# Sparse attention with routed experts on one Trainium2 core: all eight PSUM banks given out in the order's own sequence, V in five blocks per head, tokens gathered from the output, a new order

## The chip, the cores and the metric

The kernel runs on one core of one Trainium2 chip. The metric is the device time of one execution in microseconds. Before the change it is 942.32 us, the median of 3 runs (941.84 to 942.96).

## What is computed

Attention of 8 batches and 8 heads over 576 positions with head size 64, in which a score counts only if it lies within tau of its row's maximum; then a layer in which each of the 4608 tokens either passes unchanged or goes to one of 8 experts with two matrices each.

```python
# q, k, v: (8, 8, 576, 64); tau: 0.02
scores = scale * q @ k.T                      # per batch and head
scores = where(scores >= max(scores) - tau, scores, -1e9)
attn = softmax(scores);  x = attn @ v         # tokens: (4608, 512)
do_compute = x @ w_skip > 0
e_idx = argmax(x @ w_gate);  gate_w = softmax(x @ w_gate)[e_idx]
out = x
out[t] += gate_w[t] * (relu(x[t] @ w1[e]) @ w2[e])   # e = e_idx[t], if do_compute[t]
```

## The kernel before

**Stages.** Attention works on pairs of heads: 8 batches of four pairs, 32 pairs in all (g = 0 to 31). A pair has nine steps of 128 query or key positions (four for each head, and one in which the two heads' last 64 positions stand together, the tail). After attention, eight experts and one early part of the first follow as nine jobs (two layers each).

**One pair.** `plan_pair` loads q and k (L501, raw<-in_qk), splits them into a high and a low part (hl, L465/L467 and L522), and `plan_dist` and `plan_blk` spread them by DMA from SBUF to SBUF into QK (L569 to L585) and BD (L557). `plan_score` multiplies scores into PSUM (shp, L743) and takes row maxima on DVE (L748); `plan_thresh` makes the thresholds, which PE turns into rows (L838) and ACT writes into QK (L848). `plan_weights` multiplies the transposed scores less the threshold (sps, L716), takes exp on ACT (L884) and masks on DVE (p, L889); p is split into phh (ACT, L465, or DVE, L467) and phl (POOL, L926). `plan_av` multiplies them with V (avp, L954 to L958), ACT copies the result out (a), POOL divides by the sum (xb, L1006; for the tails x, L1019).

**V.** `plan_v` loads V of one batch in four DMAs (L603), takes its largest magnitude on ACT (L623), scales it (L686), rounds it to 16 bits (Vh, L689) and subtracts the rest on POOL (Vl, L692). Each head has NT = 6 blocks of 64 columns: four of 128 positions, and the last 64 positions twice, once in the lower and once in the upper half of the partitions.

**After a batch.** `plan_rows` stores the tokens of a batch (xb) in four pieces, each twice: into xs, from which the experts gather, and into out (L1125). `plan_tails` does so for the last 64 positions of two batches together (L1136). `plan_logits` makes the gate's logits on PE (L1062, L1088), `plan_gate` ranks the tokens on DVE and scatters records of token and weight into a list in HBM by POOL (lst, L1312).

**PSUM.** PSUM has eight banks of 512 float32 columns. They are dealt out for good: sps is a ring of two tiles of two banks (SPB = 2), shp a ring of two of one bank (SHB = 2), avp and gps have one bank each. The rows of the thresholds take an sps tile.

**The order.** The whole of attention and the start of the first job are not issued as written. `Plan.op` and `Plan.dma` collect operations with their dependences, an estimate of their duration for each engine that could do them and a priority; a ring (`take`, `free`) makes an operation wait for the release of the buffer it reuses. `Plan.place` goes through time greedily and picks for each engine the operation of best priority; `run` repeats that with priorities shaken by each of a list of seeds (SEEDS), each pass from the last one's times. The last pass emits the instructions in that order, and the engines then run it in order with the waits that the dependences need. The estimates know of no clock and of no contention on the DMA engines other than one common link.

**The experts.** For each job `gather_x` copies the list of token numbers (L1739, L1740) and gathers their rows from xs by indirect DMA on POOL (L454); `prep_x` turns them (L1753 to L1755), `layer1` and `layer2` or `layer2_t` multiply in three products of high and low parts (L1771, L1805, L1824), `store` scatters the result into out (L1783). `late_table` prepares a table for a loop that handles experts with more tokens than planned; on these inputs the loop is not entered.

Of the kernel before, what the change touches and what calls it, by code (L numbers as in the profile page):

```python
# [24 lines left out]
P = 128  # L25
S = 576
# [27 lines left out]
NT = NM + 2  # L54
NTP = 2 * NM + 1
STEP = 2 * NM + 1
SPB = 2
# [3 lines left out]
PFB = 3  # L61
# [19 lines left out]
GAL = {"DVE": 0.165, "POOL": 0.0}  # L81
SEEDS = (
# [11 lines left out]
class Op:  # L94
    def __init__(self, key, fn, eng, lat, off, port):
# [3 lines left out]
        self.xfer = ()  # L99

# [14 lines left out]
    def latest(self):  # L115
        r = 0.0
        for s, order in self.succ:
            x = s.rev - self.length() if order else s.rev + self.latency(s.on)
            r = x if x > r else r
        return r  # L120
# [9 lines left out]
class Plan:  # L130
    def __init__(self, tc):
        self.ops, self.rings, self.tc = [], {}, tc
        self.last = None

    def emit(self, o):
# [6 lines left out]
        nc.push_inst_callback(note)  # L142
        o.fn(e) if code.co_argcount and code.co_varnames[0] == "e" else o.fn()
# [45 lines left out]
    def place(self, links, options, ready, rank, put, lag):  # L189
# [3 lines left out]
        wait = [len(a) for a, _ in links]  # L193

# [7 lines left out]
        for _ in links:  # L202
            best = None
            for e in ENGINES:
                c = cand[e]
                if not c:
                    continue
# [9 lines left out]
            free[e] = put(i, e, t, free[e])  # L217
            if e in PEER and e in self.ops[i].port:
# [7 lines left out]

    def forward(self, rank, emit=False):
        link = 0.0

        def put(i, e, t, _):  # L230
# [7 lines left out]
            if emit:  # L238
                self.emit(o)
            return end  # L240

        self.place(self.fore, lambda i: self.opts[i], lambda i, e: self.ops[i].ready(e), rank, put, LAG)
        return max(o.t1 for o in self.ops)

    def backward(self):
        link = 0.0

        def put(i, e, t, was):
# [10 lines left out]
        ops = self.ops  # L259
        self.place(  # L260
            self.back, lambda i: (ops[i].on,), lambda i, e: ops[i].latest(), lambda i, e: -ops[i].t1, put, GAL
# [18 lines left out]
    def run(self, seeds):  # L280
        ops = self.ops
        at = {id(o): i for i, o in enumerate(ops)}
        self.opts = [[e for e in ENGINES if e in o.eng] for o in ops]
# [11 lines left out]
def attn_moe_kernel(ctx: ExitStack, tc: tile.TileContext, qk, vl, tau, wg, w1, w2, out):  # L295
# [14 lines left out]
    xs = dp.tile([NTOK, DM], F32, name="xs")  # L310
# [1770 lines left out]
```

## Time and profile before

| | us |
|---|---|
| median of 3 runs | 942.32 |
| the profiled execution | 938.75 |
| its span, first to last instruction | 937.0 |
| PE busy | 870.6 (93%) |
| DVE busy | 691.5 (74%) |
| POOL busy | 662.2 (71%) |
| ACT busy | 628.7 (67%) |

The profile is of one execution. Busy time of an engine is the time in which at least one of its instructions runs; a matmul counts from its start to its modelled end, so matmuls that follow each other closely overlap, and PE can read as busy while it could take more. Windows of the span are given as A:B in microseconds from its start. The clock is that granted to TensorE, as a share of 2.4 GHz; it has two levels, 1.2 and 2.4 GHz, so a mean between 0.50 and 1.00 is a mixture.

### The profile page before, as it was taken

What the parts mean: (1) busy time and instruction counts of PE and PEld (TensorE: products, weight loads), DVE (VectorE), ACT (ScalarE), POOL (GpSimd) and SP (SyncE); (2) the same over time, 40 slices, a digit from 0 to 9 for tenths busy, and PEclk for the clock granted to TensorE, in tenths of its full rate; (3) what the DMA queues carried; (4) which work ended last, traced back from release to release, by engine and by line L of the source; (5) the groups of instructions that cost most, each with busy time, mean ns of one, the idle gap of its engine ahead of it and who ended that gap; (6) DMA issues with size and microseconds to landing.
All of it is one profiled execution on the core that took longest, in us unless ns stands there. A gap on an engine that the chain in (4) does not pass through costs nothing. (4 is left out here: it accounts for less than half of the span.)

```text
span 937.0 us, 24810 instructions
## 1 busy us (share of the span) xinstructions
PE 870.6 (93%) x9630; PEld 808.6 (86%) x9630; DVE 691.5 (74%) x1622; ACT 628.7 (67%) x947; POOL 662.2 (71%) x452
## 2 busy tenths in 40 slices
PE   6899998998999999999998999978889999999994
PEld 3789997997999998899997898867879898999993
DVE  4888986888888888889895898967525554487770
ACT  1588986886998897899896699768414442455450
POOL 5288884896788898999987799968334545365451
PEclk8799998999999999999997999989989999999998
DMA  7987676669679759877866674623356535544530
GB/s 207 217 224 174 130 202 178 146 164 267 135 156 265 171 110 259 188 160 200 224 147 184 173 168 91 176 91 114 113 162 228 193 102 181 180 144 180 178 115 18
DMA packets 81790, 157.37 MB, mean 168 GB/s; under 512 B 28619, under 2 KB 28875, under 8 KB 81672
## 3 DMA queue, kind: packets, MB, share of 16 engines
q1 hardware_dynamic: 76984, 145.49, 59.4%
q0 software_dynamic: 4544, 10.28, 3.3%
q8 instruction: 77, 1.26, 0.5%
q14 instruction: 41, 0.34, 0.1%
q10 hardware_dynamic: 144, 0.00, 0.0%
HBM read 70.78 MB, written 24.78 MB: 102 GB/s over the span
## 5 line engine op out<-in xcount | busy, mean ns | idle before, releaser
L926 POOL TENSOR_TENSOR phl<-p,phh 128x1152 f16<-128x1152 f32 x128 | 305.4, 2394 | 58.5 <-ACT phh L465 16.1
L748 DVE TENSOR_REDUCE mx<-shp 128x1 f32<-128x288 f32 x558 | 236.7, 448 | 48.7 <-PE shp L743 45.5
L884 ACT ACTIVATE e<-sps,ntau 128x576 f32<-128x576 f32 x288 | 211.0, 740 | 57.4 <-PE sps L716 54.3
L889 DVE SCALAR_TENSOR_TENSOR p<-sps,e 128x576 f32<-128x576 f32 x288 | 215.4, 751 | 33.1 <-ACT e L884 24.9
L743 PE MATMUL shp<-QK 128*128 128x288 f32 x992 | 201.6, 314 | 6.1 <-DVE mx L748 3.2
L716 PE MATMUL sps<-QK 128*128 128x288 f32 x1024 | 191.7, 312 | 10.7 <-ACT QK L848 5.4
L716 PEld LDWEIGHTS sps<-QK 128*128 128x128 f32 x1024 | 148.7, 193 | 19.2 <-ACT QK L848 7.1
L743 PEld LDWEIGHTS shp<-QK 128*128 128x128 f32 x992 | 149.7, 191 | 12.8 <-DVE mx L748 7.8
L465 ACT ACTIVATE phh<-p 128x1152 f16<-128x1152 f32 x117 | 136.4, 1166 | 12.2 <-DVE p L889 8.1
L958 PE MATMUL avp<-Vh,phl 128*128 128x65 f16 x1280 | 130.8, 194 | 7.4 <-POOL phl L926 7.3
L954 PE MATMUL avp<-Vh,phh 128*128 128x65 f16 x1280 | 132.8, 196 | 2.6 <-ACT a L465 2.5
L957 PE MATMUL avp<-Vl,phh 128*128 128x64 f16 x1280 | 131.6, 193 | 0.0
L958 PEld LDWEIGHTS <-phl 128*128 128x128 f16 x1280 | 118.0, 98 | 8.2 <-POOL phl L926 8.1
L954 PEld LDWEIGHTS <-phh 128*128 128x128 f16 x1280 | 116.8, 98 | 8.1
L957 PEld LDWEIGHTS <-phh 128*128 128x128 f16 x1280 | 118.1, 99 | 3.0 <-issue 3.0
L1734 POOL TENSOR_TENSOR wl<-wr,wh 128x1024 fp32r<-128x1024 f32 x28 | 72.5, 2601 | 35.4 <-ACT wh L1733 30.0
L1771 PE MATMUL hps<-xh,wl 128*128 128x256 f32 (+4 forms) x256 | 77.1, 301 | 0.0
L1771 PE MATMUL hps<-xh,wh 128*128 128x256 f32 (+4 forms) x248 | 76.5, 308 | 0.1
L1771 PE MATMUL hps<-xl,wh 128*128 128x256 f32 (+4 forms) x248 | 75.0, 303 | 0.0
L1772 ACT ACTIVATE QK<-hps 128x256 fp32r<-128x256 f32 (+4 forms) x64 | 26.9, 421 | 68.9 <-PE hps L1771 68.2
L1783 POOL DMA_INDIRECT out<-o,ids x21 | 21.0, 1001 | 71.5 <-DVE o L1782 30.0
L692 POOL TENSOR_TENSOR Vl<-vraw,Vh 128x768 f16<-128x768 f32 x32 | 51.0, 1600 | 22.3 <-ACT Vh L689 22.1
(261 smaller groups left out, 1912.1 us busy)
## 6 DMA issues: line engine op xcount, KB each, us to landing
QK<-hl SPq DMA_DIRECT2D x192, 288.0 KB
wr<-in_w SPq DMA_DIRECT2D x31, 1024.0 KB
raw<-in_qk SPq DMA_DIRECT2D x32, 576.0 KB
vraw<-in_vl SPq DMA_DIRECT2D x32, 384.0 KB
xs<-xb SPq DMA_DIRECT2D x32, 256.0 KB
out<-xb SPq DMA_DIRECT2D x32, 256.0 KB
BD<-hl SPq DMA_DIRECT2D x64, 64.0 KB
xs<-x SPq DMA_DIRECT2D x8, 128.0 KB
```

Of the source, the lines that this page charges most:

```text
L465: nc.scalar.activation(dst, src, AF.Copy)
L716: nc.tensor.matmul(ps[:, j, 0:HS], w_, x_[:, js], start=(i == 0), stop=(i == len(mm) - 1))
L743: nc.tensor.matmul(ps[:, 0:HS], w_, x_[:, js], start=(q == 0), stop=(q == len(mm) - 1))
L748: nc.vector.tensor_reduce(T["mx", g][:, o, j : j + 1], T.pop(("S", g, i, j))[:, 0:HS], AX.X, ALU.max)
L884: nc.scalar.activation(e, T["W", g, i][:, :, 0:HS], AF.Exp, bias=ntau, scale=0.125)
L889: nc.vector.scalar_tensor_tensor(T[z][:, kt % 2].rearrange("p (a b) -> p a b", a=2), T.pop(("W", g, i))[:, :, 0:HS], 0.0, T.pop(("e", g, i ...
L926: nc.gpsimd.tensor_tensor(T["pl", g, i], T.pop(z)[:, 0:nk], T["ph", g, i], op=ALU.subtract)
L954: nc.tensor.matmul(pv[:, c, :], x, Vh[:, vh, kt, :], start=(j + q + c == 0), stop=False, skip_group_check=True)
L957: nc.tensor.matmul(pv[:, c, 0:D], x, Vl[:, vh, kt, :], start=False, stop=False, skip_group_check=True)
L958: nc.tensor.matmul(pv[:, c, :], y, Vh[:, vh, kt, :], start=False, stop=(c == NM), skip_group_check=True)
L1734: lo[q % 2].tensor_tensor(w[1][:, sl], rs, w[0][:, sl].bitcast(F32), op=ALU.subtract)
L1771: nc.tensor.matmul(hp_[:, 0:cap], w_, x, start=(i == 0), stop=(i == len(mm) - 1))
```

## The change

**PSUM.** The four pools become one tile of eight banks, `banks`. In `place`, each operation that takes a PSUM buffer gets a free bank, or for sps and the rows two neighbouring ones, at the moment it is placed: that which comes free first. The bank goes back when the operations that read it have been placed. A score pair may now have three instead of two buffers in flight, shp, gps and avp have no limit but the eight banks, and the rows have a kind of their own. The p ring grows from three to four. Instructions are emitted after the last pass, not during it. The backward pass knows who waits for a bank.

**V.** NT is 5: the last 64 positions stand once, in the lower half of the partitions for even heads and the upper half for odd heads.

**Tokens.** The tensor xs is gone with its stores (32 of rows, 8 of tails, one of a constant). The gathers read out. Rows of the list that hold no token are no longer clamped to a valid row: the gather leaves them out, and the two buffers that it first fills are cleared on DVE before. The gathers and the scatters of different experts are declared free of each other. The late loop masks rows that an earlier part has done; `late_table` has six more small operations for that.

**Order.** Durations of the DMAs in the plan are changed, and 50 new seeds give a new order.

```diff
-NT = NM + 2
+NT = NM + 1
-SPB = 2
+SPB = 3
-PFB = 3
+PFB = 4
+SHARED = {"shp": 0, "gps": 0, "avp": 0, "sps": 2, "row": 2}
+BANKS = 8
...
+                if name in SHARED:
+                    o.grab, o.kind = (name, len(al)), SHARED[name]
+                    if al and name == "sps":
+                        o.deps.append((al[-1], True))
+                    if name == "sps" and len(al) >= bufs:
+                        o.deps += [(x, False) for x in fr[len(al) - bufs]]
+                    al.append(o)
+                    continue
+    def open(self, units, e):
+        f = sorted(u[0][e] for u in units if u[1] == 0)
+        two = [max(u[0][e], v[0][e]) for u, v in zip(units, units[1:]) if u[1] == 0 and v[1] == 0]
+        return (f[0] if f else None, f[1] if len(f) > 1 else None, min(two, default=None))
+
+    def hold(self, o, e, units):
...
-    ps_s = att.enter_context(tc.tile_pool(name="ps_s", bufs=SPB, space=PSUM))
-    ps_h = att.enter_context(tc.tile_pool(name="ps_sh", bufs=SHB, space=PSUM))
-    ps_t = att.enter_context(tc.tile_pool(name="ps_t", bufs=1, space=PSUM))
-    ps_a = att.enter_context(tc.tile_pool(name="ps_a", bufs=1, space=PSUM))
+    ps_b = att.enter_context(tc.tile_pool(name="ps_b", bufs=1, space=PSUM))
+    banks = ps_b.tile([P, BANKS, 512], F32, name="banks")
...
-            xs[0:n, :],
+            out[0:n, :],
...
-        nc.sync.dma_start(
-            xs[NTOK - S - TL : NTOK - S, :].rearrange("p (o c) -> p o c", c=P),
-            ident[0:TL].rearrange("p (o c) -> p o c", o=1).broadcast_to([TL, DM // P, P]),
-        )
...
+    def bank():
+        return banks[:, pl.bank[0]]
+
     def sps():
-        return ps_s.tile([P, 2, 512], F32, name="sps", tag="sps")
+        a, b = pl.bank
+        return banks[:, a : b + 1 : b - a]
...
-        r = pl.op(n + OFF["tr"], rows, [o] + ring.take("sps", SPB), {PE: 0.45})
+        r = pl.op(n + OFF["tr"], rows, [o] + ring.take("row", 1), {PE: 0.45})
...
         for t in range(NM):
-            for i, dst in enumerate((xs, out)):
-
-                def st(t=t, dst=dst):
-                    r0 = b * S + t * P
-                    nc.sync.dma_start(dst[r0 : r0 + P, :], T["x", b][:, t, :])
+
+            def st(t=t):
+                r0 = b * S + t * P
+                nc.sync.dma_start(out[r0 : r0 + P, :], T["x", b][:, t, :])
...
-                for dst in (xs, out):
-                    nc.sync.dma_start(dst[r0 : r0 + TL, :], T["x2"][i * TL : (i + 1) * TL, :])
+                nc.sync.dma_start(out[r0 : r0 + TL, :], T["x2"][i * TL : (i + 1) * TL, :])
...
         nc.vector.tensor_copy(j.ids[:, 0 : j.nb], j.rec[:, 0 : j.nb, 0])
-        nc.vector.tensor_scalar(j.idg[:, 0 : j.nb], j.rec[:, 0 : j.nb, 0], float(NTOK - 1), None, op0=ALU.min)
-        j.xg = mp.tile([P, CT, DM], F32, name="xg", tag="xg")
+        j.xg = xgs.pop(0) if xgs else mp.tile([P, CT, DM], F32, name="xg", tag="xg")
         for t in range(j.nb):
             m = j.m(t)
-            gather(j.xg[0:m, t, :], j.idg[0:m, t : t + 1], NTOK)
+            gt = gather(j.xg[0:m, t, :], j.ids[0:m, t : t + 1], NTOK)
+            for x in rows:
+                tc.declare_no_dep(gt.ins, x.ins, reason="it uses no row of another expert")
+            reads.append(gt)
...
+    xgs = [mp.tile([P, CT, DM], F32, name="xg", tag="xg") for _ in range(2)]
+    for x in xgs:
+        nc.vector.memset(x, 0.0)
```

## Rows read from the trace of the kernel before

**Rows 1.** Busy time by stage; columns: stretch, length, engines' busy (operations), clock, DMA share, GB/s.

```profile
40.20:652.20 612.00, 577.88 (x7740) 545.13 (x7738) 516.88 (x1304) 507.47 (x749) 512.04 (x314) 0.98 0.71 174
652.20:697.00 44.80, 37.34 (x326) 33.81 (x324) 16.94 (x57) 13.09 (x22) 18.20 (x17) 0.89 0.39 129
697.00:925.00 228.00, 225.55 (x1442) 208.85 (x1440) 133.73 (x194) 95.13 (x160) 115.42 (x69) 1.00 0.47 160
```

**Rows 2.** The same by batch, of the exps (L884) alone: second and sixth batch.

```profile
109.00:188.10 79.10, 26.74 (x36) 0.96 0.72 175
...
416.20:488.80 72.60, 26.39 (x37) 1.00 0.77 190
```

**Rows 3.** The same by single pairs: 5, 9, 17, 21 and 24, columns as in rows 1.

```profile
125.80:151.60 25.80, 21.96 (x263) 20.96 (x263) 17.65 (x40) 15.97 (x24) 16.07 (x11) 0.90 0.92 261
208.60:231.70 23.10, 20.57 (x286) 19.13 (x282) 18.96 (x55) 15.66 (x24) 14.67 (x10) 1.00 0.99 280
358.30:380.50 22.20, 21.10 (x298) 20.19 (x295) 18.54 (x57) 16.78 (x26) 20.30 (x14) 1.00 0.98 289
433.50:451.10 17.60, 17.53 (x247) 16.66 (x246) 16.25 (x42) 14.96 (x22) 15.85 (x11) 1.00 0.88 227
488.80:517.40 28.60, 23.75 (x226) 22.64 (x226) 17.34 (x46) 18.44 (x28) 19.83 (x14) 0.78 0.63 164
```

**Rows 4.** Timeline in pair 5; columns: start, us, engine, line, operation, count, idle before.

```profile
129.71 3.07 SPq L1125 DMA_DIRECT2D out<-xb  x3
132.83 2.95 SPq L1125 DMA_DIRECT2D xs<-xb  x3
...
143.16 1.16 ACT L465 ACTIVATE hl<-raw 128x1152 fp32r<-128x1152 f32 x1 [6.29 <-DMA QK<-hl]
...
145.44 0.81 PE L716 MATMUL sps<-QK 128*128 128x288 f32 x4 [3.74 <-ACT QK L848]
```

**Rows 5.** DMA issues of the whole span: what, count, size of one.

```profile
vraw<-in_vl SPq DMA_DIRECT2D x32, 384.0 KB
xs<-xb SPq DMA_DIRECT2D x32, 256.0 KB
...
xs<-x SPq DMA_DIRECT2D x8, 128.0 KB
...
xs<-ident SPq DMA_DIRECT2D x1, 128.0 KB
```

**Rows 6.** Groups of instructions by line; after the count: busy us, mean ns, idle before.

```profile
L465 ACT ACTIVATE phh<-p 128x1152 f16<-128x1152 f32 x117 | 136.4, 1166 | 12.2 <-DVE p L889 8.1 <-POOL phl L926 1.4 <-DVE mm L793 1.2
...
L692 POOL TENSOR_TENSOR Vl<-vraw,Vh 128x768 f16<-128x768 f32 x32 | 51.0, 1600 | 22.3 <-ACT Vh L689 22.1
...
L686 ACT ACTIVATE vraw<-vraw,vmx 128x768 f32<-128x768 f32 x32 | 29.6, 939 | 0.0
...
L623 ACT ACTIVATE Vh<-vraw 128x1536 f16<-128x1536 f32 x16 | 23.7, 1484 | 16.5 <-DMA vraw<-in_vl 16.5
...
L465 ACT ACTIVATE tph<-p 128x576 f16<-128x576 f32 x27 | 18.4, 681 | 0.2
```

**Rows 7.** Waits from 40.2 to 652.2 us: who for whom, total, times, longest.

```profile
PE sps L716 <- DVE p L889: 3.5, 12, 0.4
...
PE shp L743 <- DVE mx L748: 2.9, 8, 0.9
...
PE avp L954 <- ACT a L465: 2.5, 4, 1.1
...
PE shp L743 <- DVE p L889: 2.1, 2, 1.4
```

**Rows 8.** Timeline of POOL in pair 24.

```profile
505.35 0.39 POOL L1019 TENSOR_TENSOR x<-a,z 64x128 f32<-64x128 f32 x1 [3.63 <-DMA lst<-rec,si]
```

**Rows 9.** A memset on DVE, from the groups by line (columns as in rows 6).

```profile
L359 DVE MEMSET QK<- 64x1152 f32 x2 | 2.0, 1018 | 0.4 <-issue 0.4
```

**Rows 10.** Timeline of DVE in the crossing.

```profile
684.13 0.17 DVE L1739 CAST ids<-recs 128x2 int32<-128x2 f32 x1 [5.13 <-DMA recs<-lst]
```

More of the change, by code (lines that the diff above doesn't have):

```diff
@@ L99, in __init__ @@
         self.xfer = ()
+        self.grab, self.prev, self.gives, self.then = None, [], [], []
+        self.kind = 0
+        self.bank = None
     def ready(self, e):
@@ L119, in latest @@
             r = x if x > r else r
+        for s in self.then:
+            x = s.rev + self.latency(s.on)
+            r = x if x > r else r
         return r
@@ L132, in __init__ @@
         self.ops, self.rings, self.tc = [], {}, tc
-        self.last = None
+        self.last = self.bank = None
     def emit(self, o):
@@ L205, in place @@
                 c = cand[e]
+                if units:
+                    open_ = self.open(units, e)
+                    c = [
+                        x if ops[x[2]].grab is None else (max(x[0], open_[ops[x[2]].kind]), x[1], x[2])
+                        for x in c
+                        if ops[x[2]].grab is None or open_[ops[x[2]].kind] is not None
+                    ]
                 if not c:
@@ L225, in place @@
                     add(q)
+    def open(self, units, e):
[3 more added lines that the diff above has]
+    def hold(self, o, e, units):
+        if o.grab:
+            if o.kind < 2:
+                us = sorted((u for u in units if u[1] == 0), key=lambda u: u[0][e])[0 : o.kind + 1]
+            else:
+                us = [(u, v) for u, v in zip(units, units[1:]) if u[1] == 0 and v[1] == 0]
+                us = list(min(us, key=lambda x: max(x[0][0][e], x[1][0][e])))
+            name, k = o.grab
+            o.bank, o.prev = sorted(u[2] for u in us), []
+            for u in us:
+                o.prev += u[3]
+                u[3] = self.rings[name][1][k]
+                u[0], u[1] = dict.fromkeys(ENGINES, 0.0), len(u[3])
+            self.where[o.grab] = us
+        for g in o.gives:
+            for u in self.where[g]:
+                u[1] -= 1
+                for q in ENGINES:
+                    u[0][q] = max(u[0][q], o.t1 + o.latency(q))
     def forward(self, rank, emit=False):
         link = 0.0
+        self.where = {}
+        units = [[dict.fromkeys(ENGINES, 0.0), 0, n, ()] for n in range(BANKS)]
         def put(i, e, t, _):
@@ L730, in score @@
             if ps is None:
-                T["S", g, i, j] = ps = ps_h.tile([P, 512], F32, name="shp", tag="shp")
+                T["S", g, i, j] = ps = bank()
             if M:
@@ L854, in plan_trow @@
             T["thr", g, h] = xs_[-1]
-        ring.free("sps", xs_)
+        ring.free("row", xs_)
         ring.free("nh", [r])
@@ L973, in plan_av @@
             if NM not in kts:
-                ring.free("ph", [x]) if NM + 1 not in kts else ring.free("tp", [x])
+                ring.free("ph", [x])
+            elif h:
+                ring.free("tp", [x])
         def cpy(e):
@@ L1481, in half @@
         def half():
-            return ps_h.tile([P, 512], F32, name="shp", tag="shp")
+            return bank()
         def xt(a):
@@ L1716, in attn_moe_kernel @@
     tab = cp.tile([1, 2 * NOV + 1], I32, name="tab")
+    done = cp.tile([1, NOV], F32, name="done")
     NK = E + 1
-    rows = []
+    rows, reads = [], []
     def split_w(src, raws=(), lo=(nc.vector, nc.gpsimd)):
@@ L1790, in store @@
         )
-        for x in rows:
+        for x in rows + reads:
             tc.declare_no_dep(sc.ins, x.ins, reason="every token goes to one expert")
```

134 lines of the change are left out of this document (83 added, 51 removed), and 10 rows, old and new, of the table SEEDS.

## The prediction

> **What bounds the kernel now.** I read the page first, then the table by stage, the same table by batch and by single pair of heads, then the timeline where a pair is slow, and the list of waits last. The table by stage shows three parts that matter: attention from 40.2 to 652.2 us (612 us), the crossing into the experts (44.8 us) and the experts (228 us), in which PE is busy 225.6 us [rows 1]. The experts are bound by PE's own work, which the change leaves alone; whatever it is worth must show in the 612 us and the crossing.
>
> In attention no engine is the bound by itself. PE reads 578 of 612 us busy, DVE 517, POOL 512, ACT 507, and the DMA engines 0.71 of their time [rows 1]. PE's figure overstates it, since its matmuls overlap. The reader should see four engines at 83% and more, tied by short waits, so that the time is set by how well the written order dovetails them. Cut into batches of four pairs (36 exps, L884), the second batch takes 79.1 us and the sixth 72.6 [rows 2].
>
> The slow places are at the batch boundaries. A quiet pair takes 17.6 us (433.5 to 451.1). Pairs 5, 9 and 17, each right after a batch has ended, take 25.8, 23.1 and 22.2 us, at DMA shares of 0.92, 0.99 and 0.98 [rows 3]. So these three lose 8.2 + 5.5 + 4.6 = 18.3 us against a quiet pair. What fills the DMA engines is seen in the timeline around pair 5: the row stores of the finished batch, twice each (xs and out), go out from 128 to 136 us; the next pair's loads and QK spreads queue behind them, ACT sits idle 6.29 us for a QK<-hl to land so that an hl buffer comes free, and PE idles 3.74 us behind ACT [rows 4]. After that gap the granted clock is low for a while (the pair's mean is 0.90, [rows 3]), which lengthens the loss. Pair 24 is slow for another reason: POOL waits 3.63 us for a scatter to land [rows 8], and its 28.6 us run at a mean clock of 0.78 [rows 3].
>
> **The change part by part.**
>
> Tokens gathered from out. Per batch four stores of 256 KB vanish (xs<-xb), and per two batches two of 128 KB (xs<-x) [rows 5]: 1.05 MB per batch, 1.31 MB where the tails go too. At the rates that the slow pairs reached (261, 280 and 289 GB/s, [rows 3]) that is 4.0, 4.7 and 4.5 us of full DMA engines. V in five blocks takes 64 KB from each of four loads of 384 KB [rows 5], 0.26 MB or 0.9 to 1.0 us per batch. Together the three boundaries can give back up to 4.0 + 4.7 + 4.5 + 2.8 = 16.0 us, which is less than the 18.3 they lose, so it could all pass through; at least nothing does, if another wait stands right behind. I take half, 8, since the order is new and DMA bursts may be packed again. SP also issues 40 DMAs fewer, about 1 us each at such a boundary (three xs stores take it 2.95 us, [rows 4]); these issues stand ahead of the next pair's loads in SP's queue, so up to 4 us of the 16 may come through SP and not through the DMA engines: it is the same time, not more of it. The other four boundaries inside attention I count as giving nothing.
>
> V in five blocks, on the engines. 64 ACT operations shrink from 768 to 640 columns and 16 from 1536 to 1280. ACT's own slope is seen in L465: 1152 columns 1.166 us, 576 columns 0.681 us, so 0.84 ns a column; that gives 64 x 0.108 + 16 x 0.216 = 10.4 us. POOL's 32 subtractions (L692, 1.600 us) can shrink by a sixth at most, 8.5 us [rows 6]. Both engines are near 83% in a stage where four engines wait for each other, so between none and all of the 10.4 reaches the end; I take a quarter, 2.5.
>
> All banks from one pool, three score pairs in flight, four p buffers. The chip's instructions stay the same; what can go are PE's waits for a bank to be read out. The trace has them in four rows: sps for the mask 3.5 us, shp for the maximum 2.9, avp for its copy 2.5, shp (held up by the mask, in DVE's order) 2.1, in all 11.0 us [rows 7]. Between 0 and 11 comes back; more only if PE's running ahead feeds ACT and DVE better, which no row prices; I take 4.5. The fourth p buffer removes waits of DVE for POOL, a single short event; nothing.
>
> New order. It moves everything, and its waits can't be read from this trace. What a bad event costs can: pair 24 took 28.6 - 17.6 = 11.0 us more than a quiet pair, from one wait of 3.63 us [rows 3, 8]. Whether a new order has more or fewer of such events than this one is open in both directions; I put it at zero in the sum, and at one event either way, 11 us, in the range.
>
> The crossing. Two memsets of 1536 columns are new on DVE, ahead of the first list of tokens. One of 1152 columns takes 1.018 us [rows 9], so two take 2.7 us; DVE idles 5.13 us there, waiting for the records to load [rows 10], so they cost nothing, and 2.7 us if that cover were gone. One small DVE operation goes. Rows past the count are no longer gathered, which can only shorten a gather. Half the last stores go, but PE then reaches the first gathered tokens no earlier than their list, so I count 0.5 (0 to 2). In the start, V's shorter loads and the dropped 128 KB store [rows 5] save 0.39 MB, 1.5 us at 261 GB/s, beside a chain that runs through QK and not V; between 0 and 1.5, I take 0.5. The new operations of the late table (some six tiny ones on DVE) stand beside PE-bound matmuls: nothing.
>
> Sum: 8 + 2.5 + 4.5 + 0.5 + 0.5 = 16 us off the profiled execution, 938.75 us (937.0 of span and 1.75 around it): 922.75. The median of the runs shown, 942.32, stands 3.57 above that execution; so 926.3, rounded to 926.
>
> **The rivals.**
>
> Everything works: the boundaries give the whole 16.0, the banks 11, the V work 5, and crossing and start 2. That is 34 us, 908. For it speaks that the sixth batch already runs in 72.6 us with a DMA share of 0.77 [rows 2]; eight batches at that pace would take 581 us of the stage's 612. Against it: four engines over 83% don't all dovetail.
>
> The DMA is hidden anyway: the stores go, but ACT and PE wait at the boundaries for something else that was late too (V's preparation on ACT and POOL falls in the same pairs). Then only the V work and part of the banks remain, some 4 us: 938. For it speaks that pair 17 lost 4.6 us with hardly any listed wait for a DMA.
>
> No change: the same with a little lost elsewhere, 942.
>
> Slower: the new order leaves gaps ahead of PE, and the clock falls after them. The mechanism is that of pair 24: a short wait of PE's feeders (there POOL, in the scatters), then matmuls at the lower of the two levels, 1.2 GHz (the pair's mean is 0.78), 11 us in all [rows 3, 8]. The place is wherever the order puts a scatter or a load just before work that PE needs. It decides from the second further event on: two cost 22 against a gain of 16 (948), three 33 (959). In the steady stretch from 433.5 to 451.1 PE is busy 17.53 of 17.6 us at a clock of 1.00 under the fixed rings [rows 3], so the gaps would have to be new. The Trainium skill has a rule that speaks for this rival and against the change: TensorE: Matmul & The Clock Gate, section "A second HAM failure mode: psum-queue depth-cycling", tells of a kernel that cycled through PSUM banks, left PE small idles between groups, and so had its clock swing between the two levels. By that rule the steady pairs themselves would lose clock; by the row they have no idles to speak of, and more free banks should leave fewer.
>
> That the change doesn't do what it says: the banks are now one tile, and if waits were kept for the tile and not for the bank, each of 288 score pairs would wait for its exp, 0.74 us (26.74 over 36, [rows 2]), 214 us in all, and as long again for the mask. That each buffer is a slice by bank number speaks against it; 1 in 100.
>
> **How the numbers follow.** Forecast (918 to 934) 0.48; everything works 0.15; hidden anyway (934 to 940.4) 0.15; no change 0.05; slower 0.17, the tile case in it. About 0.2%, 1.9 us, is what a measurement of this kernel can tell from no change. Faster: 0.48 + 0.15 + 0.15 = 0.78; same 0.05; slower 0.17. The range runs from 905, below the case in which everything works, to 946, so that about half of the slower case lies outside; the forecast's own range is 918 to 934.
>
> **What would show it.** Right: no xs stores; the pairs after a batch's end at 18 to 21 us, with ACT's hl no longer waiting 6 us for QK<-hl; attention ending some 15 us earlier than 652; fewer PE waits for DVE's maximum and mask; the experts from first to last matmul within 1 us of 228. Wrong: DMA share still above 0.9 and slow pairs at the boundaries; clock well below the 0.98 of attention [rows 1]; PE waits on banks as before; or gaps of several us in POOL behind scatters in more places.

## The result and the profile after

The changed kernel takes 909.49 us (median of 4 runs, 909.11 to 910.36) where the kernel before takes 942.08: a ratio of 0.9668, 95% interval 0.9629 to 0.9707, or 32.6 us less. The forecast was 926, its range 905 to 946. So the direction was right, and the gain forecast, 16 us, was half of the one measured. The profiled execution is 909.38 us, its span 907.6 against 937.0.

The table by stage, cut at the first exp, the last exp, and the first and last matmul of the experts (columns as in [rows 1], which it answers to):

```profile
27.30:624.90 597.60, 572.59 (x7759) 545.62 (x7758) 503.63 (x1298) 510.47 (x763) 521.40 (x326) 0.98 0.66 167
624.90:667.50 42.60, 34.73 (x322) 31.16 (x321) 19.21 (x58) 14.34 (x25) 19.20 (x17) 0.92 0.23 69
667.50:895.60 228.10, 226.19 (x1447) 209.31 (x1445) 128.93 (x196) 95.31 (x160) 117.62 (x69) 1.00 0.48 162
```

| part of the span, us | before | after | difference |
|---|---|---|---|
| until the first exp | 40.2 | 27.3 | -12.9 |
| attention | 612.0 | 597.6 | -14.4 |
| crossing | 44.8 | 42.6 | -2.2 |
| experts | 228.0 | 228.1 | +0.1 |
| end | 12.0 | 12.0 | 0.0 |

The stage that I had priced, attention, gives what I had forecast for it (15: boundaries 8, V's work 2.5, banks 4.5). Almost as much again came ahead of it, in the start, where I had counted 0.5. The cut at the first exp flatters the start, though: batch 0 then takes 73.4 us where it took 68.8, so that at its end (100.7 for 109.0) the lead is 8.3 us and not 12.9.

The second and the sixth batch (exps alone, answering to [rows 2]), and pairs 5, 9, 17, 21 and 24 (answering to [rows 3]):

```profile
100.70:171.60 70.90, 26.17 (x37) 1.00 0.69 172
394.00:462.70 68.70, 26.07 (x36) 1.00 0.75 183
```

```profile
117.00:136.70 19.70, 19.70 (x319) 18.98 (x319) 16.22 (x39) 15.98 (x25) 18.93 (x14) 1.00 0.86 226
187.90:204.30 16.40, 16.25 (x241) 15.54 (x241) 15.64 (x35) 13.46 (x21) 14.82 (x10) 1.00 0.84 230
337.50:356.40 18.90, 18.31 (x254) 17.65 (x254) 15.14 (x38) 15.92 (x22) 18.56 (x13) 1.00 0.91 233
410.60:427.70 17.10, 17.10 (x248) 16.63 (x247) 15.51 (x40) 14.26 (x20) 15.92 (x10) 1.00 0.86 224
462.70:492.30 29.60, 26.30 (x341) 25.35 (x340) 19.61 (x51) 20.50 (x34) 25.02 (x18) 0.94 0.56 151
```

The three boundary pairs fell from 71.1 us together to 55.0 and their DMA shares to 0.84 to 0.91; the quiet pair stayed near 17; pair 24 is as slow as ever. The reader should look at the number of matmuls too (the first x of a line): pair 24 holds 341 now and held 226 before. A new order moves work from pair to pair, so the length of a pair can't be compared across orders without that count.

The waits of PE for a bank, from the waits of the stretch 27.3 to 624.9 (answering to [rows 7]):

```profile
PE banks L811 <- DVE mx L816: 3.3, 4, 1.8
...
PE banks L784 <- DVE p L957: 3.1, 7, 0.7
...
PE banks L1022 <- DVE p L957: 2.0, 2, 1.8
...
PE banks L811 <- DVE p L957: 1.6, 4, 0.8
...
PE banks L784 <- DVE mx L816: 0.8, 1, 0.8
```

The four rows of before made 11.0 us. Three of them are here, with 8.0, and that of avp for its copy is gone. But two are new: the product with V (L1022) now waits for the mask, and the weights' scores (L784) for the maximum, since each may be given a bank that the other kind has just left. With them it is 10.8 us, so the waits gave back next to nothing.

The start is new. PE's timeline from its first scores to the thresholds (nh), first before, then after:

```profile
18.86 0.58 PE L743 MATMUL sps<-QK 128*128 128x288 f32 x1 [4.72 <-DMA QK<-hl]
21.68 4.20 PE L743 MATMUL sps<-QK 128*128 128x288 f32 x15 [2.24 <-DMA QK<-hl]
26.79 0.37 PE L640 MATMUL gps<-ident,vmx 128*1 128x128 f32 x1 [0.91 <-DVE vmx L636]
27.27 2.26 PE L743 MATMUL sps<-QK 128*128 128x288 f32 x8
...
37.69 0.22 PE L838 MATMUL sps<-identr,nh 128*66 128x128 f32 x1
```

```profile
14.15 2.77 PE L811 MATMUL banks<-QK 128*128 128x288 f32 x16
18.74 2.40 PE L811 MATMUL banks<-QK 128*128 128x288 f32 x16 [1.82 <-DVE mx L829]
...
24.41 0.29 PE L906 MATMUL banks<-identr,nh 128*66 128x128 f32 x1 [2.47 <-DVE nh L887]
...
25.87 0.37 PE L704 MATMUL banks<-ident,vmx 128*1 128x128 f32 x1 [0.54 <-DVE vmx L700]
```

Before, the first scores wait for QK spreads, and batch 0's maximum of V (vmx) is turned in the middle of pair 0's scores; the thresholds (nh), which need the same bank gps, come after it. After, the scores start 4.7 us earlier, the thresholds come first, and V's maximum is turned behind them.

The clock has a large share in it, too. From the first score to the end of pair 0's last, first before, then after (columns as in [rows 1]):

```profile
18.86:33.74 14.88, 11.40 (x40) 9.41 (x40) 7.87 (x16) 4.32 (x5) 0.00 (x0) 0.50 1.06 250
```

```profile
14.15:21.94 7.79, 5.95 (x40) 5.22 (x38) 6.25 (x14) 0.00 (x0) 2.00 (x30) 1.00 0.99 249
```

Both hold the 38 matmuls of pair 0's scores and two others. Before, PE waits 4.72 us for a spread and then runs all of them at the lower level of the clock; after, at the upper one. So the 12.9 us are 4.7 of a later start, 7.1 of a longer stretch, in which PE is busy 5.45 us more, and 1.1 behind it.

### The profile page after: what moved, and what is told of

Same layout as the page of the kernel before. It is cut to its first block, busy times and chain, and to the rows that moved or that the text cites. A ratio compares the mean times of both kernels' runs of the same rounds, so it can differ in the third digit from the quotient of the medians.

```text
span 907.6 us, 24647 instructions
## 1 busy us (share of the span) xinstructions
PE 854.5 (94%) x9630; PEld 800.4 (88%) x9630; DVE 669.6 (74%) x1601; ACT 626.6 (69%) x957; POOL 671.6 (74%) x463
## 5 line engine op out<-in xcount | busy, mean ns | idle before, releaser
L816 DVE TENSOR_REDUCE mx<-banks 128x1 f32<-128x288 f32 x558 | 229.3, 447 | 39.0 <-PE banks L811 34.8
L957 DVE SCALAR_TENSOR_TENSOR p<-banks,e 128x576 f32<-128x576 f32 x288 | 214.5, 751 | 40.7 <-ACT e L952 35.2
L952 ACT ACTIVATE e<-banks,ntau 128x576 f32<-128x576 f32 x288 | 207.6, 738 | 37.6 <-PE banks L784 29.1
L811 PE MATMUL banks<-QK 128*128 128x288 f32 x1024 | 193.4, 308 | 7.9 <-DVE mx L816 3.3
L784 PE MATMUL banks<-QK 128*128 128x288 f32 x1024 | 186.5, 311 | 5.2 <-DVE p L957 3.1
L811 PEld LDWEIGHTS banks<-QK 128*128 128x128 f32 x1024 | 149.6, 190 | 13.3 <-DVE mx L816 4.5
L784 PEld LDWEIGHTS banks<-QK 128*128 128x128 f32 x1024 | 149.0, 193 | 10.5 <-DVE p L957 6.7
L1022 PE MATMUL banks<-Vh,phh 128*128 128x65 f16 x1280 | 132.1, 196 | 2.0 <-DVE p L957 2.0
L1026 PE MATMUL banks<-Vh,phl 128*128 128x65 f16 x1280 | 130.4, 194 | 2.4 <-POOL phl L994 2.4
L1025 PE MATMUL banks<-Vl,phh 128*128 128x64 f16 x1280 | 130.9, 193 | 0.9 <-POOL Vl L756 0.9
L1022 PEld LDWEIGHTS <-phh 128*128 128x128 f16 x1280 | 116.7, 98 | 7.6
L1801 POOL TENSOR_TENSOR wl<-wr,wh 128x1024 fp32r<-128x1024 f32 x28 | 74.9, 2688 | 34.8 <-ACT wh L1800 29.3
L586 POOL TENSOR_TENSOR hl<-raw,hl 128x576 fp32r<-128x576 f32 x45 | 64.2, 1437 | 27.4 <-DVE hl L535 17.9
## 6 DMA issues: line engine op xcount, KB each, us to landing
QK<-hl SPq DMA_DIRECT2D x192, 288.0 KB
```

Source lines behind the costliest of these rows:

```text
L784: nc.tensor.matmul(ps[:, j, 0:HS], w_, x_[:, js], start=(i == 0), stop=(i == len(mm) - 1))
L811: nc.tensor.matmul(ps[:, 0:HS], w_, x_[:, js], start=(q == 0), stop=(q == len(mm) - 1))
L816: nc.vector.tensor_reduce(T["mx", g][:, o, j : j + 1], T.pop(("S", g, i, j))[:, 0:HS], AX.X, ALU.max)
L952: nc.scalar.activation(e, T["W", g, i][:, :, 0:HS], AF.Exp, bias=ntau, scale=0.125)
L957: nc.vector.scalar_tensor_tensor(T[z][:, kt % 2].rearrange("p (a b) -> p a b", a=2), T.pop(("W", g, i))[:, :, 0:HS], 0.0, T.pop(("e", g, i ...
L1022: nc.tensor.matmul(pv[:, c, :], x, Vh[:, vh, kt, :], start=(j + q + c == 0), stop=False, skip_group_check=True)
```

## The experiments

Each kernel is compared with the kernel before run on the same chip, whose medians there were 939.7 to 940.9 us; differences in us are the ratio times that median. The orders are the written ones unless it is said.

**The second stores, put back and taken away.** In the changed kernel:

```diff
-                nc.sync.dma_start(out[r0 : r0 + P, :], T["x", b][:, t, :])
+                for dst in (xs, out):
+                    nc.sync.dma_start(dst[r0 : r0 + P, :], T["x", b][:, t, :])
```

> The changed kernel with its order kept, but every row store and tail store made twice again: once to out and once to a DRAM tensor that nobody reads. 40 more DMAs on SP, 1.05 MB per batch and 1.31 MB with the tails, 10.5 MB in all less what falls at the end. Theory A, that the second stores cost time where batches end: the pairs after a batch's end (19.7, 16.4 and 18.9 us in the changed kernel for pairs 5, 9 and 17) grow again by 3 to 6 us each, and the whole becomes 8 to 16 us slower, 917 to 925 us. Rival B, that the transfers were hidden and the gain there came from the order or the banks: within 2 us of 909.5. If it costs far more than 16 us, an order made for one store suffers more from two than an order made for two.

917.97 us, a ratio of 0.9737 (0.9681 to 0.9794) where the changed kernel has 0.9668: 6.5 us by the ratios, 8.5 by the medians. Pair 17 grew by 3.8 us and pair 5 by 0.5; the largest growth was in pair 10, from 21.6 to 26.6. In the kernel before, the stores into out left out:

```diff
                 for dst in (xs, out):
-                    nc.sync.dma_start(dst[r0 : r0 + P, :], T["x", b][:, t, :])
+                    if dst is xs:
+                        nc.sync.dma_start(dst[r0 : r0 + P, :], T["x", b][:, t, :])
```

> The kernel before with its order kept, but each row and tail stored once, into the tensor that the experts gather from, and not into out (so tokens that no expert touches stay unwritten in out). 40 DMAs fewer on SP. Theory A, that the second stores cost time where batches end: pairs 5, 9 and 17 (25.8, 23.1 and 22.2 us) fall to 18 to 21 us, and the whole becomes 8 to 16 us faster, 926 to 934 us. Rival B, that the transfers were hidden, or that an order made for two stores can't use the room: within 2 us of 942.

933.93 us, 0.9929 (0.9894 to 0.9963), or 6.7 us less (3.5 to 10.0). Pair 5 fell from 25.8 to 21.2 and pair 9 from 23.1 to 21.3, pair 17 stayed at 22.3. (The 10.5 MB of the first expectation are too much: 32 stores of 256 KB and 8 of 128 KB make 9.4.) Both ways the second stores are worth 6 to 9 us, at or just under the lower edge of Theory A. Rival B falls.

**V in five blocks.** In the kernel before, loads and operations cut to five of six blocks:

```diff
-                nc.scalar.activation(Vh[2 * q // HV][:, at, :, 0:D], T["vr", b][:, hs], AF.Copy)
+                nc.scalar.activation(Vh[2 * q // HV][:, at, 0 : NM + 1, 0:D], T["vr", b][:, hs, 0 : NM + 1], AF.Copy)
```

> The kernel before with its order kept, but V loaded, rounded and split in five blocks per head instead of six: ACT's and POOL's operations on V shrink by a sixth and each batch loads 0.26 MB less (the tail of odd heads uses the even heads' rows, so those rows of the result are other numbers; the work of the matmuls is unchanged). My term for the engines was 2.5 us of at most 10.4, and the loads were put at 0.9 to 1.0 us for each of three batches: Theory A 2 to 6 us faster, 936 to 940 us. Rival B, that ACT and POOL are no bound where V is prepared: within 1 us of 942. Rival C, that four engines near 83% pass on all of it: 10 us or more, 932 or less.

Its total, 964.33 us, says nothing of V: other tokens go to other experts, and the loop for crowded experts, which the kernel before never enters, runs here for a further 44 us behind them (the groups by line from 640 us on):

```profile
L2022 PE MATMUL lhp<-lxT,wa 128*128 128x128 f32 x64 | 9.6, 325 | 0.8 <-ACT lxT L2015 0.8
```

I had not thought of that when I wrote the expectation. Attention has no such choice in it. It took 607.9 us for 612.0, so 4.1 less, in Theory A's bounds; it is a difference between single executions.

**V's loads behind the QK spreads**, in the kernel before:

```diff
+        vs = [o for o in out if o in self.behind[0]]
+        last = max(out.index(o) for o in self.behind[1])
...
+        at = min(last, use - 1)
...
+        moved = [o for o in out[: at + 1] if o not in vs] + vs
+        out[: at + 1] = moved
...
+    pl.behind = (T["vl0"], T["qk", 0, 0] + T["qk", 0, 1] + [T["bd", 0]])
```

> The kernel before, whole result, with the four V loads of batch 0 moved behind pair 0's QK spreads and block copy in SP's queue; all else in the old order. In the kernel before these loads stand between the spreads, PE waits 4.72 us and then 2.24 us for a spread, and the first exp begins at 40.2 us; in the changed kernel the spreads come first and it begins at 27.3 us. Theory A, that V's loads ahead of the spreads cost the start: the first exp begins 5 to 10 us earlier and the whole becomes 4 to 10 us faster, 932 to 938 us. Rival B, that the start is set by the chain through PE, DVE and ACT in the old order: first exp less than 2 us earlier. Rival C, that the start is won and V then comes late and gives it back in batch 0: first exp 5 us earlier or more, the whole within 2 us of 942.

942.16 us, 1.0037 (0.9997 to 1.0077), and the first exp at 46.1 us, 5.9 later and not 5 earlier. PE's timeline in it says why:

```profile
15.36 0.37 PE L759 MATMUL sps<-QK 128*128 128x288 f32 x1 [1.82 <-DMA QK<-hl]
...
32.64 0.37 PE L656 MATMUL gps<-ident,vmx 128*1 128x128 f32 x1 [12.20 <-DVE vmx L652]
```

The scores did start 3.5 us earlier, and then PE stood 12.20 us before the turn of V's maximum, which its order has ahead of the remaining scores. My Theory A saw only one of two things in line, the loads. Behind them stands the chain of V. Rival B, which put the start down to the old order, comes nearer, though it expected no loss.

**Is it the order?** Four kernels with orders searched afresh, in the same way and for 20 to 25 minutes (9, 7, 8 and 24 accepted steps): the kernel before; the changed kernel with the old fixed rings; with shared banks but two score pairs and three p buffers; and as it is.

```diff
-SHARED = {"shp": 0, "gps": 0, "avp": 0, "sps": 2, "row": 2}
+SHARED = {}
+FIXED = {"sps": ((0, 1), (2, 3)), "shp": ((4,), (5,)), "gps": ((6,),), "avp": ((7,),)}
...
+                if name in FIXED:
+                    o.bank = FIXED[name][len(al) % bufs]
```

> The kernel before, whole result, but with another order: the planner's own search was run afresh from its first order for 25 minutes, and its 9 accepted steps stand in the place of the 49. Its planned end is 668.6 us against 661.4 for the kernel before. It shows how far the time hangs on the order alone, and is the yardstick for the next three runs, whose orders were searched in the same way. If the plan's differences come through one to one: 942 + 7 = 949 us. If the order is as decisive as I put it in the prediction (one slow event more or less is 11 us): anywhere from 938 to 960.

> The changed kernel, whole result, with one store per row and V in five blocks and four p buffers, but with the fixed rings of the kernel before (two pairs for the scores, two banks for the maxima, one for the small things, one for a) and an order searched afresh for 25 minutes; planned end 666.8 us. Against the run of the kernel before with its own fresh order (planned 668.6) it shows stores and V without the banks. Theory A, that the banks are the larger half of the gain and stores and V give about 11 us (6.6 for the stores and 4 for V were measured with the orders kept): 10 to 14 us below that run, 935 to 940 us, and some 20 us above the next runs with shared banks. Rival B, that the gain came from a better order found by a longer search, and the banks give little: within 5 us of the run with all banks shared and a fresh order.

> The changed kernel, whole result, with its banks shared, but only two score pairs in flight and three p buffers as before, and an order searched afresh for 20 minutes; planned end 656.0 us, 10.8 less than with fixed rings and 5.5 more than with three pairs and four buffers. Theory A1, that what counts is that the single banks for small things and for a are no longer handed on in the order of writing: 9 to 13 us below the run with fixed rings. Rival A2, that the third score pair is what counts: within 4 us of the run with fixed rings.

> The changed kernel, whole result, unchanged but for an order searched afresh for 25 minutes (24 accepted steps for 50; planned end 650.5 us against 644.9). Theory A, that the banks carry the gain and not the search: 909.5 + 6 = 915 us, 908 to 922, and some 20 us or more below the run with fixed rings. Rival B, that the order that was handed in was a find: 925 us or more. With the kernel before in its own fresh order it gives the change's worth a second time, in another pair of orders: 33 us if the change itself carries it.

| kernel, fresh order | us | ratio (95%) | first exp | attention | clock of the span |
|---|---|---|---|---|---|
| before | 940.36 | 1.0005 (0.9974 to 1.0036) | 36.3 | 608.9 | 0.971 |
| fixed rings | 917.53 | 0.9774 (0.9728 to 0.9820) | 35.4 | 593.7 | 0.983 |
| shared, two pairs, three p | 924.64 | 0.9837 (0.9792 to 0.9883) | 28.3 | 607.3 | 0.970 |
| shared, as changed | 912.83 | 0.9726 (0.9689 to 0.9763) | 29.5 | 597.6 | 0.975 |

Attention in them, in that order (columns as in [rows 1]):

```profile
36.30:645.20 608.90, 576.28 (x7719) 542.24 (x7717) 512.69 (x1285) 505.86 (x745) 522.00 (x322) 0.98 0.71 174
```

```profile
35.40:629.10 593.70, 571.27 (x7767) 538.30 (x7766) 514.14 (x1299) 501.40 (x752) 507.26 (x317) 1.00 0.65 163
```

```profile
28.30:635.60 607.30, 575.98 (x7779) 547.16 (x7778) 521.59 (x1313) 498.80 (x750) 509.36 (x318) 0.97 0.65 161
```

```profile
29.50:627.10 597.60, 573.05 (x7730) 542.29 (x7731) 511.42 (x1296) 510.19 (x765) 521.55 (x326) 0.98 0.66 166
```

Three things follow. The order of before is no find: a fresh one gave 940.4 us (not the 949 of its planned end). That of the changed kernel is worth 3.3 us by the medians (5.5 by the ratios) against a fresh one, and the change is worth 27.5 us in the pair of fresh orders. The start goes by the banks: 40.2, 36.3 and 35.4 us in three orders with fixed rings, 27.3, 28.3 and 29.5 in three with shared banks, and two score pairs are enough for it. But Theory A's other half, that the banks carry the larger part of the whole, fell: with fixed rings 917.5 us, 4.7 from the run with shared banks and not 20, within the 5 us of Rival B there. The run with shared small banks, which has one p buffer fewer, is 7 us slower than fixed rings and not 9 to 13 faster, though the plan had it 10.8 ahead. In attention shared banks gave nothing over fixed rings (597.6 against 593.7).

**All but the banks**, with the order of before kept: one store, five blocks (tails in halves, as in the change), four p buffers.

```diff
-                T[z] = ap_.tile([P, 2, S], F32, name="p", tag="p", bufs=PFB)
+                T[z] = ap_.tile([P, 2, S], F32, name="p", tag="p", bufs=PFB + 1)
```

> The kernel before with its order and its fixed rings kept, but with everything else that the change does to the queues: one store per row and tail (into the tensor that the experts gather from, so tokens that no expert touches stay unwritten in out), V in five blocks with the tails of odd heads in the other half (full result for V), and four p buffers. Measured alone with the order kept, the stores gave 6.7 us and V 4.1 us of attention. Theory A, additive and the fourth p buffer worth nothing: 10 to 12 us faster than the kernel before, 930 us, attention 601 us from 612. Rival B, that the fourth p buffer, which I counted at nothing, carries part of the gain: 16 us or more, 926 or less. Rival C, that they share one gain: 5 to 8 us, 935. What then is left to 909.5 is the shared banks and the order made with them.

931.46 us, 0.9910 (0.9875 to 0.9945), or 8.5 us less (5.2 to 11.8):

```profile
37.80:638.90 601.10, 573.36 (x7740) 542.29 (x7739) 513.78 (x1304) 499.84 (x749) 505.21 (x314) 0.98 0.67 160
```

Attention is 601.1 us, 10.9 less, as Theory A had it. The start is 2.4 us shorter, too, and what follows attention 3.2 longer (288.0 for 284.8 us, in single executions). The total lies between A and C. The fourth p buffer adds nothing that can be seen; Rival B falls, as long as the order is one made for three.

**The start alone**, in the kernel before:

```diff
-            T["vt", b] = g_tile()
+            T["vt", b] = ps_a.tile([P, 4, P], F32, name="avp", tag="avp") if b == 0 else g_tile()
...
+            out[: at + 1] = [o for o in out[: at + 1] if o in need] + [o for o in out[: at + 1] if o not in need]
```

> The kernel before, whole result, its order kept from the first exp on. In it pair 0's thresholds take the single bank for small things after batch 0's maximum of V has used it, so V's loads and its whole chain stand ahead of the first exp. Here that chain of batch 0 uses the bank of a instead, and all that the first exp doesn't need is put behind it in every queue. Theory A, that the fixed ring of one bank for small things is what makes the start late (40.2 us before, 27.3 in the changed kernel; 36.3 and 35.4 in two other orders with fixed rings, 28.3 and 29.5 in two with shared banks): the first exp begins at 27 to 31 us, and the whole becomes 4 to 10 us faster, 932 to 938 us. Rival B, that V's chain, now behind the exps, holds up the first AV and gives it all back: first exp as early, but the whole within 2 us of 941.

949.64 us, 1.0099 (1.0065 to 1.0132), so 9.3 us slower. The first exp began at 31.7 us, just above the 27 to 31 of Theory A, and the gain was then lost twice over; ACT's timeline:

```profile
31.71 0.74 ACT L899 ACTIVATE e<-sps,ntau 128x576 f32<-128x576 f32 x1 [1.18 <-PE sps L729]
42.07 0.17 ACT L679 ACTIVATE vmx<-avp 128x1 f32<-128x1 f32 x1 [4.59 <-PE avp L673]
...
51.29 0.74 ACT L899 ACTIVATE e<-sps,ntau 128x576 f32<-128x576 f32 x1 [2.87 <-PE sps L729]
```

Between the first and the second exp lie 19.6 us: PE, ACT and DVE all had V's chain next in their queues and waited through it, and pair 0 took 34.7 us for 16.2. So the ring of one bank, with the order of the queues that it forces (the edit undoes both), is what makes the first exp late. Freeing it pays only in an order that spreads V's chain among the exps, as the changed kernel's does.

**What makes pair 24 slow.** I had read it as a short wait of POOL for its scatters, followed by a low clock, 11 us in all. In the changed kernel that wait is there again, so the product that waits was moved, first to DVE and then to ACT, at its place in the order.

```diff
-            nc.gpsimd.tensor_tensor(
+            nc.vector.tensor_tensor(
                 T["x2"].rearrange("p (h d) -> p h d", d=D)[rs, 2 * hp : 2 * hp + 2],
```

> The changed kernel, whole result, its order kept, but the tail's product (x <- a,z, 32 operations of 0.4 us on POOL) runs on DVE at the same place. On POOL it waits for scatters to land: 2.3 us in pair 13 and 2.7 us in pair 24, and PE waits 3.3 us for it there before the clock falls to 0.57 (pair 24 takes 29.6 us against 17.1 for a quiet one). Theory A, that these waits make the slow pairs, as I read it in the kernel before: pair 24 falls to 18 to 22 us, and the whole becomes 6 to 14 us faster than the changed kernel, 896 to 904 us. Rival B, that pair 24 is slow for want of other work (the rows of the gate, V's preparation) and the wait is only where it shows: pair 24 stays at 26 us or more, the whole within 3 us of 909.5. DVE gets 32 times some 0.2 us, 6 us in all, which could cost up to that.

920.24 us, 0.9782 (0.9734 to 0.9830): 10.7 us slower than the changed kernel by the ratios. Pair 24 did fall, to 25.9 us, but the product took 0.92 us in the mean on DVE and not 0.27. The timeline of DVE and POOL where it took longest:

```profile
326.57 4.32 DVE L1089 TENSOR_TENSOR x<-a,z 64x128 f32<-64x128 f32 x1
327.08 1.34 POOL L756 TENSOR_TENSOR Vl<-vraw,Vh 128x640 f16<-128x640 f32 x1
328.38 2.35 POOL L994 TENSOR_TENSOR phl<-p,phh 128x1152 f16<-128x1152 f32 x1
```

It ends at 330.89, 0.16 us after the second of these POOL operations. 32 of them held DVE for 29.4 us, 20 more than at 0.27 each. Neither theory has this time: pair 24 stays 0.1 us short of Rival B's bound, and the whole is slower than both.

```diff
+            for h in range(2):
+                c = (2 * hp + h) * D
+                nc.scalar.activation(
+                    T["x2"][rs, c : c + D], T["a", g][rs, h, NM, 0:D], AF.Copy, scale=T["z", g][rs, h, NM : NM + 1]
+                )
```

> The changed kernel, whole result, its order kept, with the tail's product on ACT (two operations of 64 columns with the factor as a scale, some 0.2 us each) in the place of one on POOL. On DVE the same product took 0.27 us at best and 0.92 in the mean, up to 4.3 beside POOL's work, and cost more than it brought; pair 24 fell from 29.6 to 25.9 us all the same. Theory A, that POOL's waits for the scatters at that product make the slow pairs: without them, and without DVE's load, pair 24 falls to 18 to 24 us and the whole becomes 4 to 10 us faster than the changed kernel, 900 to 905 us. Rival B, that a product moved to any engine costs its place in an order made without it, and pair 24 stays slow for other work: pair 24 at 25 us or more, the whole 908 to 916 us.

908.35 us, 0.9658 (0.9619 to 0.9697), against 0.9668 for the changed kernel: no difference that these runs resolve. Pair 24 in it, then the last 8.3 us of pair 24 in the changed kernel, then the last 14.4 us in the kernel before (columns as in [rows 1]):

```profile
460.80:485.90 25.10, 25.03 (x342) 23.77 (x339) 19.15 (x51) 21.73 (x38) 24.16 (x16) 1.00 0.65 178
```

```profile
484.00:492.30 8.30, 5.43 (x29) 5.26 (x30) 1.84 (x4) 3.14 (x8) 7.41 (x6) 0.78 0.45 158
```

```profile
503.00:517.40 14.40, 11.61 (x55) 11.45 (x56) 5.47 (x14) 4.51 (x7) 9.16 (x7) 0.57 0.72 223
```

Without POOL's wait 342 matmuls (341 in the changed kernel) run in 25.1 us with PE busy throughout and the clock at 1.00. So in the changed kernel the wait and the low clock after it cost 29.6 - 25.1 = 4.5 us, and the other 8 us by which pair 24 exceeds a quiet pair are work: over a third more matmuls (342 to 248). The 4.5 us don't reach the end. Batch 6 is 2.9 us shorter and batch 7 3.1 longer. Rival B holds.

## Why the prediction was right and where it failed

**Boundaries (8) and V on the engines (2.5): right.** Their sum, 10.5, was measured at 8.5 (5.2 to 11.8) with the order kept, of which the stores are 6 to 9 and V about 4 of attention. That half of the bound of 16 comes through, and not all of it, was the right choice, though for it I had no better reason than that DMA bursts may pack again. The fall of the three boundary pairs by 16.1 us looks like the whole bound, and it isn't: putting the stores back took 6.5 to 8.5 us. In pairs 9 and 17 part of the rest is work that the new order has elsewhere (241 matmuls for 286, and 254 for 298). Pair 5 has more of it (319 for 263) and is 6.1 us shorter all the same, with the clock at 1.00 for 0.90.

**Banks in the steady stretch (4.5 of 11.0): not borne out.** The waits that the term was read from gave back 0.2 us. From all-but-the-banks to the changed kernel attention went from 601.1 to 597.6 us, 3.5 less; between the fresh orders it went the other way, 3.9 more. For the whole, shared banks with a third score pair gave 4.7 us between two fresh orders. That is the size I had put down, but it came ahead of the first exp, where I had not looked for it, so the size was luck.

**New order (0, with 11 either way): the term most mis-sized.** For the kernel before, zero was right: a fresh order moved it by 0.05%. But an order made for the change has worth of its own. From all-but-the-banks in the old order (0.9910) to fixed rings in an order made for them (0.9774) there are 12.8 us, though the tokens' new path and the plan's new durations are in that step as well; the longer search gave 5.5 more by the ratios (0.9726 to 0.9668). With the 8.5 of stores and V and 4.5 of the banks that makes the 31 us by which the ratios fell, and the sum had nothing for more than half of it. The price of a bad event, 11 us, took a quiet pair as the measure for pair 24. In the kernel before that may be near, since pair 24 had fewer matmuls than a quiet pair (226 against 247); it wasn't tried there. In the new order the event costs 4.5, and that is given back later.

**Start (0.5, between 0 and 1.5): here the mechanism failed.** The prediction says that V's shorter loads lie "beside a chain that runs through QK and not V". The chain does run through V: the turn of V's maximum stands in PE's queue ahead of 22 of the 38 matmuls of pair 0's scores, and the thresholds may take the one gps bank only when V's chain has left it. PE's timeline of the first 40 us shows it in one line (26.79, gps<-ident,vmx), and I never opened that stretch, since my table of stages began at the first exp. Over three orders each, fixed rings begin their exps at 35.4 to 40.2 us and shared banks at 27.3 to 29.5. I had priced the banks by PE's waits for a bank between 40.2 and 652.2 us. What fixed rings cost here is no such wait: the single bank is handed on in the order in which the program asks for it, and the planner may not turn that round. But the first exp is not the end. At the start of the 36th, the last of batch 0, the lead over the kernel before has gone from 12.9 to 8.3 us, that over all-but-the-banks from 10.5 to 5.6, and that between the two fresh orders from 5.9 to 3.7, with the same number of matmuls done in each of these to within 5 of some 990. With 8.3 us in place of 0.5 the sum would have been 23.8, or 918.5; the start does not carry the missing 16 us alone.

**Crossing (0.5, 0 to 2): 2.2, just above its range;** the experts are within 0.1 us, as said.

**The rivals.** "The DMA is hidden anyway" fell with both runs on the stores. "Everything works" gave 908 and is close to the number for another reason: its banks and boundaries in full did not come, an early start and a better order did. That the time lies inside the range is owed to this case, which set the range's lower end, and so in part to luck. "Slower" didn't happen: pairs with a low clock are still there (24, 25 and 30 as before, and now pair 0), but those behind the first boundary (5 and 6) are gone, and there are no more of them. The rule of the Trainium skill, TensorE: Matmul & The Clock Gate, section "A second HAM failure mode: psum-queue depth-cycling", did not show itself: pair 21 has PE busy 17.10 of 17.1 us at clock 1.00 with the banks shared, and attention's clock is 0.98 in both kernels.

**What stays open.** From all-but-the-banks in the old order (0.9910) to the changed kernel (0.9668) there are 22.8 us by the ratios, 19.3 by the spans: 10.5 of start, 3.5 of attention, 5.3 behind it. But fixed rings with an order made for one store, five blocks and four p buffers already reach 917.5, 13 to 14 us below the same rings in the old order. Here are the first six batches, the seventh and the eighth of all-but-the-banks, then the same of fixed rings (columns as in [rows 1]):

```profile
37.80:474.00 436.20, 427.60 (x5855) 406.09 (x5854) 386.32 (x967) 374.28 (x561) 371.40 (x228) 1.00 0.73 173
474.00:558.40 84.40, 77.51 (x950) 73.18 (x948) 64.69 (x180) 64.13 (x97) 67.01 (x44) 0.92 0.62 146
558.40:638.90 80.50, 68.25 (x939) 63.02 (x938) 62.77 (x158) 61.44 (x93) 66.80 (x43) 0.96 0.39 104
```

```profile
35.40:479.20 443.80, 430.95 (x5860) 407.87 (x5859) 389.67 (x971) 380.98 (x571) 367.68 (x227) 1.00 0.69 171
479.20:558.60 79.40, 74.81 (x978) 69.65 (x977) 64.66 (x177) 61.13 (x93) 74.96 (x50) 0.98 0.62 157
558.60:629.10 70.50, 65.51 (x934) 60.78 (x932) 59.82 (x153) 59.29 (x91) 64.61 (x42) 1.00 0.41 116
```

The new order's gain in attention lies in the last two batches alone, 15.0 us, where the old order has a low clock and the new one hardly; in the six before them it is 7.6 us longer. The changed kernel has 82.5 and 79.7 us there, at 0.94 and 0.96, so it lacks this gain. Whether an order made for the change avoids such stretches because the DMA engines are less full or by luck, one order of each kind can't tell. Nor do the runs separate the third score pair from the fourth p buffer in the 11.8 us between shared small banks and the kernel as changed, or that buffer from the order in the 7 us between fixed rings and shared small banks.

## What to carry to other kernels

Open the start of the span as carefully as its steady part: a chain that ends in the first step of the main loop is bare, and a buffer ring of one that is handed on in the order of writing can tie two chains together that have nothing to do with each other, without a wait that any list of waits would name as its cost. Price each part of a change with the order kept (one edit at a time in the old order) before believing pair by pair differences between two orders, and count the work in a stretch before calling it slow. But give the order a term of its own in the sum: one made for the change was worth more here (12.8 us, from one such order) than any single part of it. And read a gain at the end of a stage in which all kernels have done the same work, not at its first step. An edit to the head of a queue is only worth what the engines find next in theirs: moving loads or chains by hand in an order made without it cost 0 to 9 us here, where a planner free to choose gained 7 to 13 at the first exp.

## What the runs showed of the hardware

A 64x128 product of two SBUF tiles on DVE, 0.27 us by itself, took up to 4.32 us while POOL ran its own products back to back. SBUF — State Buffer in the Trainium skill, section "SBUF: two separate sides", says that such an operation and one of POOL exclude each other for the whole instruction; the trace agrees, and adds that the loser here sat out more than one POOL operation (it ended 0.16 us after the second of those shown). With no POOL operation beside it the product took 0.27 to 0.29 us.

On POOL the same product waited 2.3 to 3.6 us for scatters that POOL itself had issued before it, in both kernels ([rows 8] is one of them). On DVE and on ACT no such wait is listed. The wait is for a semaphore that the product's instruction carries on POOL, so it is one of the program's, and not shown to be the chip's; what in the program ties that product to the scatters, the runs don't show.
